# Attention logits of a windowed-attention and gated-MLP kernel summed by accumulating DMAs instead of selector matmuls

## The chip, the cores and the metric

The kernel runs on one core of a Trainium2 chip. The metric is the device time of one execution in microseconds (us). Each kernel was run several times. "Span" is the profiled part of one execution; it is some 2 to 3 us shorter than the time. PE is TensorE, DVE VectorE, ACT ScalarE, POOL GpSimd, SP the engine that issues most DMAs. A name such as L485 is a line of the kernel in question; the line numbers differ from kernel to kernel.

## The reference

```python
# x: 2048 tokens x 640;  32 heads of 20;  window of 8 keys, 2 apart
xn  = layernorm(x)
q, k, v = split_heads(xn @ wqkv)
logits[h, s, w] = sum_d q[h, s, d] * k[h, s - 2*w, d] / sqrt(20)      # -1e9 where s - 2w < 0
attn = softmax(logits, over w)
o[h, s, d] = sum_w attn[h, s, w] * v[h, s - 2*w, d]
out = x + o @ wo + ((xn @ w_gate) * (xn @ w_up)) @ w_down
```

## The kernel before

Tokens lie along the free dimension. The 640 columns of q, k and v are 5 chunks of 128 partitions, permuted so that partition p of every chunk belongs to head p // 4. A head's logit is therefore a sum over 5 chunks and over 4 neighbouring partitions ("head rows"). DVE multiplies q by the shifted k, for two window offsets (a "pair") at a time, and adds two chunks to two others. PE then adds the last three chunks and the four head rows at once, with a 0/1 selector G:

```python
def qk_steps(h, p, s):                 # h: half of the tokens, p: pair of window offsets
    ...                                # prod(): one DVE multiply for both offsets of the pair
    a, b = kept[:, :, 0:NCH - NKC, :], tmp[:]            # NCH = 5 chunks, NKC = 3 stay
    return [ (..., prod(kept, 0, NKC)), (..., prod(tmp, NKC, NCH)), (..., a = a + b on DVE) ]

def qk_logits(h, batch):               # two pairs at a time
    for p, s in batch:
        for c in range(NKC):
            for q in range(NSB):       # 4 blocks of 256 tokens, 32 PSUM partitions each
                e.matmul(PS[32*q:32*q+32, lb, :], G[:], SL[s][:, :, c, q*SB:(q+1)*SB], ...)
    ...                                # ACT copies the bank to LOG, scaled

def attn_move(h):                      # softmax weights back to 128 partitions: 16 DMAs a half
    for r in range(4):
        for q in range(NSB):
            dma(ATB[h][r:128:4, q], LOG[h][32*q:32*q+32])
```

Every engine is one queue, filled once, in program order. While it is built, two counters, `t_pe` and `t_dve`, estimate how far PE and DVE are; the projections, the gated products and the output tiles ("fill") are put between the attention steps by these estimates. `pv(b)` is the attention-times-value work for block b of 256 tokens, on DVE; an output tile t may be queued when `pv(t // 2)` has been:

```python
batch(0, [pair(0, 0), pair(0, 1)]);  batch(0, [pair(0, 2), pair(0, 3)])
...  b0 = pair(1, 0);  softmax head of half 0;  batch(1, [b0, pair(1, 1)]);  softmax rest;  attn_move(0)
batch(1, [pair(1, 2), pair(1, 3)])
pv(0);  settle();  head of softmax 1;  pv(1);  rest of softmax 1;  attn_move(1);  pv(2) ... pv(7)
```

The down-projection weight WD lies in the same memory as the products, so it is loaded only when these have been read. The gated products need USX, a ring of six buffers.

## Time and profile before

| | before |
|---|---|
| time, median of 4 | 262.12 us |
| PE busy / DVE busy, of a span of 260.7 us | 98% / 83% |
| stalls of PE from 31 to 258 us | 0.91 us |
| selector matmuls in the chain | 5.1 us |

The table of engines of the kernel before (busy us, share of the span, instructions), and its slices 2 (tenths of 40 slices of the span; PEclk is the granted clock of PE):

```profile
PE 255.6 (98%) x1669; PEld 150.7 (58%) x1669; DVE 216.1 (83%) x240; ACT 107.3 (41%) x193; POOL 6.7 (3%) x13
...
PE   7999999899999999999999999999999999999996
...
DMA  6968889400000275065001376000311000021301
```

PE is full, or nearly so, from the second slice to the last but one, so only work taken from PE, or a stall, can move the time much. The timeline of PE where the first two groups of selector matmuls stand (start, us, engine, line, what; in brackets the idle time before it and what ended it):

```profile
47.61 0.83 PE L485 MATMUL PS<-SL,G 128*32 128x512 f16 x12
49.35 0.83 PE L485 MATMUL PS<-SL,G 128*32 128x512 f16 x12 [0.91 <-DVE SL L475]
50.11 14.22 PE L424 MATMUL PS<-XNT,WQKV 128*128 128x512 bf16 x65
```

Twelve selector matmuls, placed on four quarters of the array, take only 0.83 us together. The chain that ended last holds them in four pieces (start, us, what):

```profile
49.35 0.83 PE PS L485 x12
...
64.34 1.44 PE PS L485 x24
...
86.41 1.41 PE PS L485 x24
...
110.59 1.41 PE PS L485 x24
```

They sum to 5.1 us; with the stall of 0.91 us, 6.0 us are to be won.

### The profile page before, as it was taken

The numbers are of one execution on the slowest core, as the hardware profiler recorded it, in microseconds if no ns is written. First come the engines' busy times: TensorE is split into PE (matmuls) and PEld (weight loads), VectorE is DVE, ScalarE is ACT, GpSimd is POOL, SyncE is SP. The second block draws the span as 40 slices with busy tenths as digits, with TensorE's granted clock in tenths as the row PEclk, the third lists the DMA queues.
The fourth block names the chain that finished last, engine by engine and source line by source line (L and its number), as shares of the span: only waits on it lengthen the run. The fifth ranks groups of instructions, "written<-read, shape, count | busy, mean of one in ns | idle before, by whom it ended". The sixth has DMA issues, their size and how long they took to land.

```text
span 260.7 us, 4018 instructions
## 1 busy us (share of the span) xinstructions
PE 255.6 (98%) x1669; PEld 150.7 (58%) x1669; DVE 216.1 (83%) x240; ACT 107.3 (41%) x193; POOL 6.7 (3%) x13
## 2 busy tenths in 40 slices
PE   7999999899999999999999999999999999999996
PEld 3899855354554444444467744446774444777775
DVE  5799889999999999998847999999999999422221
ACT  3565558555657555565630035551004555000000
POOL 2000050000200000000000000000000000000000
DMA  6968889400000275065001376000311000021301
GB/s 202 326 136 148 100 226 402 156 3 0 0 3 0 50 206 144 0 208 219 3 0 57 97 199 175 0 4 0 99 54 50 0 3 0 27 74 53 101 28 50
DMA packets 21922, 23.46 MB, mean 90 GB/s; under 512 B 9872, under 2 KB 19472, under 8 KB 21904
## 3 DMA queue, kind: packets, MB, share of 16 engines
q1 hardware_dynamic: 21760, 23.04, 31.2%
q8 instruction: 13, 0.21, 0.3%
q10 hardware_dynamic: 144, 0.16, 0.2%
q14 instruction: 5, 0.04, 0.0%
HBM read 14.42 MB, written 2.62 MB: 65 GB/s over the span
## 4 chain that ended last, share of the span: by engine, by line
PE 80%; DVE 14%; SPq 2%; DMA 2%; ACT 1%; issue 1%
PE PS L577 40%; PE PS L608 28%; PE PS L424 10%; DVE SL L467 3%; SPq L283 2%; DVE XNS L371 2%; PE PS L485 2%; DVE STATS L354 2%; DVE SL L475 2%; DVE TMP L467 2%; DVE STATS L348 2%; DMA XST<-in_A_x_dram 2%; DVE MV L360 1%; DVE SD L369 1%; ACT KH L451 0%
## 5 line engine op out<-in xcount | busy, mean ns | idle before, releaser
L577 PE MATMUL PS<-XNT,WG 128*128 128x512 bf16 x240 | 59.6, 379 | 0.0
L577 PE MATMUL PS<-XNT,WU 128*128 128x512 bf16 x240 | 59.6, 379 | 0.0
L608 PE MATMUL PS<-WD,HT 128*128 128x320 bf16 (+1 forms) x396 | 57.6, 295 | 0.0
L579 ACT ACTIVATE HT<-PS 128x512 bf16<-128x512 f32 x48 | 28.7, 598 | 58.2 <-PE PS L577 58.2
L608 PEld LDWEIGHTS PS<-WD,HT 128*128 128x128 bf16 x396 | 38.1, 98 | 14.7
L551 DVE TENSOR_TENSOR PVB<-VO,ATB 128x10240 f16<-128x10240 bf16 x8 | 43.9, 5488 | 0.1
L424 PE MATMUL PS<-XNT,WQKV 128*128 128x512 bf16 x200 | 43.9, 379 | 0.0
L612 DVE TENSOR_TENSOR FOUT<-PS,XR 128x320 bf16<-128x320 f32 (+1 forms) x33 | 15.5, 477 | 30.4 <-PE PS L608 30.1
L577 PEld LDWEIGHTS PS<-XNT,WU 128*128 128x128 bf16 x240 | 23.4, 98 | 28.5 <-issue 0.4
L577 PEld LDWEIGHTS PS<-XNT,WG 128*128 128x128 bf16 x240 | 23.4, 98 | 28.2 <-issue 0.4
L579 ACT ACTIVATE USX<-PS 128x512 bf16<-128x512 f32 x48 | 28.7, 597 | 22.2 <-PE PS L577 20.8
L424 PEld LDWEIGHTS PS<-XNT,WQKV 128*128 128x128 bf16 x200 | 23.3, 118 | 20.2 <-issue 0.8
L546 DVE TENSOR_TENSOR PVB<-PVB 128x5120 f16<-128x5120 f16 (+1 forms) x16 | 34.4, 2150 | 0.0
L467 DVE TENSOR_TENSOR SL<-QH,KH 128x6144 f16<-128x6144 bf16 x8 | 26.8, 3352 | 1.4 <-ACT KH L451 1.4
L608 PE MATMUL PS<-WO,VO 128*128 128x320 bf16 (+1 forms) x165 | 27.1, 295 | 0.0
L582 DVE TENSOR_TENSOR HT<-HT,USX 128x512 bf16<-128x512 bf16 x48 | 18.5, 417 | 4.2 <-ACT USX L579 4.2
L608 PEld LDWEIGHTS PS<-WO,VO 128*128 128x128 bf16 x165 | 15.9, 98 | 5.9
L475 DVE TENSOR_TENSOR SL<-SL,TMP 128x4096 f16<-128x4096 f16 x8 | 18.3, 2290 | 0.2
L467 DVE TENSOR_TENSOR TMP<-QH,KH 128x4096 f16<-128x4096 bf16 x8 | 18.4, 2302 | 0.0
L430 ACT ACTIVATE VO<-PS 128x512 bf16<-128x512 f32 x20 | 11.9, 597 | 9.8 <-PE PS L424 9.8
L437 PE MATMUL PS<-XNT,WQKV 128*128 128x128 bf16 x200 | 12.6, 220 | 0.2
L437 PEld LDWEIGHTS PS<-XNT,WQKV 128*128 128x128 bf16 x200 | 11.6, 118 | 1.2 <-DVE XNT L394 0.5
(49 smaller groups left out, 137.8 us busy)
## 6 DMA issues: line engine op xcount, KB each, us to landing
ATB<-LOG SPq DMA_DIRECT2D x32, 128.0 KB, 2.6
XR<-in_A_x_dram SPq DMA_DIRECT2D x16, 160.0 KB, 2.3
XST<-in_A_x_dram SPq DMA_DIRECT2D x15, 160.0 KB, 3.9
out_dram<-FOUT SPq DMA_DIRECT2D x15, 160.0 KB, 1.8
WG<-in_B_w_gate_dram SPq DMA_DIRECT2D x1, 1920.0 KB, 9.5
WU<-in_B_w_up_dram SPq DMA_DIRECT2D x1, 1920.0 KB, 13.8
WD<-in_B_w_down_dram SPq DMA_DIRECT2D x1, 1920.0 KB, 8.2
WQKV<-in_A_wqkv_dram SPq DMA_DIRECT2D x10, 160.0 KB, 3.8
```

The lines of the kernel that those rows point to most:

```text
L424: op("pe", (lambda l, x, c: lambda e: e.matmul(PS[:, b, :], l, x, start=(c == 0), stop=(c == NCH - 1)))(l, x, c), r=[l, x], w=[PS[:, b, :] ...
L430: op("act", lambda e: e.activation(o, PS[:, b, :], ACT.Copy), r=[PS[:, b, :]], w=[o], name=f"pev{which}_{m}_{j}")
L437: op("pe", (lambda o, l, x, st, sp: lambda e: e.matmul(o, l, x, start=st, stop=sp))(o, l, x, st, sp), r=[l, x], w=[o], name=f"pp{which}_{m ...
L467: return lambda: op("dve", lambda e: e.tensor_tensor(o[:], qw, kw, ALU.mult), r=[q, k], w=[o[:]], name=f"prod{h}_{p}_{c0}")
L475: lambda: op("dve", lambda e: e.tensor_tensor(a, a, b, ALU.add), r=[a, b], w=[a], name=f"psum{h}_{p}")),
L546: return lambda: op("dve", lambda e: e.tensor_tensor(o, x, y, ALU.add), r=[x, y], w=[o], name=f"{name}_{b}")
L551: lambda: op("dve", lambda e: e.tensor_tensor(PVB[:], vw, aw, ALU.mult), r=[v, a], w=[PVB[:]], name=f"pv_{b}")),
L577: op("pe", (lambda l, x, c: lambda e: e.matmul(PS[:, b, :], l, x, start=(c == 0), stop=(c == NCH - 1)))(l, x, c), r=[l, x], w=[PS[:, b, :] ...
L579: op("act", lambda e: e.activation(o, PS[:, b, :], ACT.Copy), r=[PS[:, b, :]], w=[o], name=f"guev{which}_{m}_{j}")
L582: h_pending.append(lambda: op("dve", lambda e: e.tensor_tensor(h, h, o, ALU.mult), r=[h, o], w=[h], name=f"h{m}_{j}"))
L608: op("pe", (lambda l, x, i, b: lambda e: e.matmul(PS[:, b, 0:wid], l, x, start=(i == 0), stop=(i == n - 1)))(l, x, i, b), r=[l, x], w=[PS[ ...
L612: op("dve", (lambda o, xr, b: lambda e: e.tensor_tensor(o, PS[:, b, 0:wid], xr, ALU.add))(o, xr, b), r=[PS[:, b, :], xr], w=[o], name=f"fi ...
```

## The change

Its intent: free PE of the selector matmuls. DVE writes its products token block by token block in FP16; two accumulating DMAs of 512 KB add chunks to the first product; a plain copy of head row 0 and three accumulating DMAs of head rows 1 to 3 (128 KB each) build the logits, now 32 heads times 4 token blocks on 128 partitions. Each of the six must wait for the one before. The weights go back by 4 DMAs a half with a repeated source. The attention scale moves into the copy of q, the mask becomes an addition, and the softmax is FP16. The diff, cut to its core:

```diff
-    NKC = 3
-    NSL = 3
-    SL = [sb(f"SL{s}", [128, 2, NKC, HS], FP16) for s in range(NSL)]
+    PSB = [128, NSB, 2, SB]
+    PP = [sb(f"PP{s}", [128, 2] + PSB[1:], FP16, at=a_pr + ...) for s in range(2)]   # in WD's memory
+    PE_ = [ five buffers for the first product, three of them in PVB's memory ]
...
-        return [ prod(kept, 0, NKC), prod(tmp, NKC, NCH), a + b ]          # 2 multiplies
+        return prod(first, 4, 1) + prod(a, 0, 2) + prod(b, 2, 2) + [ a + b ]   # 6 multiplies
+    def acc(o, i, name):
+        op("pool", lambda e: e.dma_start(o, i, accum_op=ALU.add), r=[o, i], w=[o], dma=True, name=name)
+    def qk_chain(h, p, s, en):
+        return [
+            lambda: acc(first[:], slot[:, 0], f"acc{h}_{p}_0"),
+            lambda: acc(first[:], slot[:, 1], f"acc{h}_{p}_1"),
+            lambda: dma(dst, row(0), r=[first[:]], w=[dst], name=f"row{h}_{p}_0"),
+            lambda: acc(dst, row(1), f"row{h}_{p}_1"),
+            lambda: acc(dst, row(2), f"row{h}_{p}_2"),
+            lambda: acc(dst, row(3), f"row{h}_{p}_3"),
+        ]
-    def qk_logits(h, batch):   ... selector matmuls, LOG evictions, mask ...
...
     def pair(h, p):
         ... DVE steps ...
+        ch[0]();  held[0]();  ch[1]();  held[1]()        # held: rows 2 and 3 of the pair before
+        ch[2]();  ch[3]();    held[:] = ch[4:]
...
     pv(0)
-    settle()
+    pv(1)
+    settle(b_end + 15.0)
     for it in headB: step(it)
-    pv(1)
     for it in restB: step(it)
```

More of the change, by code (lines that the diff above doesn't have):

```diff
@@ L26 @@
 EPS = 1e-5
-NEG = -1e9
+NEG = -30000.0
 VP = 32
@@ L232, in build_kernel @@
     a_pr = place[0]
-    NKC = 3
-    NSL = 3
-    WD = sb("WD", [128, NF, D], at=a_pr)
-    WO = sb("WO", [128, NCH, D], at=a_pr + NF * D * 2)
-    SL = [sb(f"SL{s}", [128, 2, NKC, HS], FP16) for s in range(NSL)]
-    PVB = sb("PVB", [128, NCH, W, SB], FP16, at=place[0] - 2 * NKC * HS * 2)
-    TMP = sb("TMP", [128, 2, NCH - NKC, HS], FP16)
+    WD = sb("WD", [128, NF, D])
+    WO = sb("WO", [128, NCH, D])
+    PSB = [128, NSB, 2, SB]
+    PP = [sb(f"PP{s}", [128, 2] + PSB[1:], FP16, at=a_pr + 2 * s * HS * 4) for s in range(2)]
+    PE_ = [sb("PE0", PSB, FP16, at=a_pr + 4 * HS * 4)]
+    a_pv = place[0]
+    PVB = sb("PVB", [128, NCH, W, SB], FP16)
+    TMP = sb("TMP", [128, 2] + PSB[1:], FP16, at=a_pv)
+    for s in range(3):
+        PE_.append(sb(f"PE{s + 1}", PSB, FP16, at=a_pv + (2 + s) * HS * 4))
     XNT = sb("XNT", [128, NCH, S])
@@ L243, in build_kernel @@
     for h in range(2):
-        ATB.append(sb(f"ATB{h}", [128, NSB, W, SB], at=place[0]))
+        ATB.append(sb(f"ATB{h}", [128, NSB, W, SB], FP16, at=place[0]))
+        if h == 0:
+            PE_.append(sb("PE4", PSB, FP16, at=place[0] + NSB * W * SB * 2))
         QH.append(sb(f"QH{h}", [128, NCH, HS]))
@@ L250, in build_kernel @@
     a_log = place[0]
-    LOG = [sb(f"LOG{h}", [128, W, SB]) for h in range(2)]
-    M1 = sb("M1", [128, 4, SB])
-    M2 = sb("M2", [128, 2, SB])
-    M3 = sb("M3", [128, SB])
+    LOG = [sb(f"LOG{h}", [128, W, SB], FP16) for h in range(2)]
+    M1 = sb("M1", [128, 4, SB], FP16)
+    M2 = sb("M2", [128, 2, SB], FP16)
+    M3 = sb("M3", [128, SB], FP16)
     S1 = sb("S1", [128, 4, SB], FP16)
@@ L276, in build_kernel @@
     IDENT = sb("IDENT", [128, 128])
-    G = sb("G", [128, H], FP16)
+    MASK = sb("MASK", [128, W, PAD], FP16)
+    MSK0 = sb("MSK0", [128, W, PAD], FP16)
     PS = nc.alloc_psum_tensor("PS", [128, 8, 512], FP32)
@@ L291, in build_kernel @@
        r=[IDENT[:]], w=[IDENT[:]], name="ident")
-    op("pool", lambda e: e.memset(G[:], 0.0), w=[G[:]], name="g0")
-    op("pool", lambda e: e.affine_select(G[:], G[:], pattern=[[-4, H]], compare_op=ALU.is_gt,
-                                         fill=1.0, base=-3, channel_multiplier=1),
-       r=[G[:]], w=[G[:]], name="g1")
-    op("pool", lambda e: e.affine_select(G[:], G[:], pattern=[[-4, H]], compare_op=ALU.is_ge,
-                                         fill=0.0, base=0, channel_multiplier=1),
-       r=[G[:]], w=[G[:]], name="g2")
     op("pool", lambda e: e.memset(KH[0][:, :, 0:PAD], 0.0), w=[KH[0][:, :, 0:PAD]], name="kpad")
     op("pool", lambda e: e.memset(VO[:, :, 0:VP], 0.0), w=[VO[:, :, 0:VP]], name="vpad")
+    op("pool", lambda e: e.memset(MASK[:], 0.0), w=[MASK[:]], name="mask0")
+    op("pool", lambda e: e.memset(MSK0[:], 0.0), w=[MSK0[:]], name="msk0")
+    op("pool", lambda e: e.affine_select(MSK0[:], MSK0[:], pattern=[[DIL, W], [1, PAD]], compare_op=ALU.is_ge, fill=NEG,
+                                         base=-PAD, channel_multiplier=0), r=[MSK0[:]], w=[MSK0[:]], name="msk1")
     def x_load(t, eng="sp"):
@@ L326, in late_loads @@
     def late_loads():
+        dma(MASK[0:128:4], MSK0[0:32], r=[MSK0[0:32]], w=[MASK[0:128:4]], name="mask")
         wqkv_load(2)
@@ L429, in proj @@
             o = qk_dst(which, m, j * JB, JB)
-        op("act", lambda e: e.activation(o, PS[:, b, :], ACT.Copy), r=[PS[:, b, :]], w=[o], name=f"pev{which}_{m}_{j}")
+        sc = SCALE if which == 0 else 1.0
+        op("act", lambda e: e.activation(o, PS[:, b, :], ACT.Copy, scale=sc), r=[PS[:, b, :]], w=[o],
+           name=f"pev{which}_{m}_{j}")
     def proj_part(which, t, ms, b, col):
@@ L450, in part_evac @@
         i = PS[:, b, col:col + nm * nt * TS].rearrange("p (m s) -> p m s", m=nm)
-        op("act", lambda e: e.activation(o, i, ACT.Copy), r=[PS[:, b, :]], w=[o], name=f"ppev{which}_{m0}_{t0}")
+        sc = SCALE if which == 0 else 1.0
+        op("act", lambda e: e.activation(o, i, ACT.Copy, scale=sc), r=[PS[:, b, :]], w=[o], name=f"ppev{which}_{m0}_{t0}")
     def k_seam():
@@ L455, in k_seam, with qk_steps @@
         op("pool", lambda e: e.tensor_copy(o, i), r=[i], w=[o], name="kseam")
-    def qk_steps(h, p, s):
-        kept, tmp = SL[s], TMP
+    def qk_steps(h, p, s, en):
+        slot, first = PP[s], PE_[en]
         kp = KH[h][:, 0, 0:1].ap[0]
-        def prod(o, c0, c1):
-            q = QH[h][:, c0:c1, :]
-            k = KH[h][:, c0:c1, 4 * p:4 * p + HS + 2]
-            kw = bass.AP(k.tensor, k.offset, [kp, [2, 2], [KL, c1 - c0], [1, HS]])
-            qw = q.unsqueeze(1).to_broadcast([128, 2, c1 - c0, HS])
-            return lambda: op("dve", lambda e: e.tensor_tensor(o[:], qw, kw, ALU.mult), r=[q, k], w=[o[:]],
-                              name=f"prod{h}_{p}_{c0}")
-        a, b = kept[:, :, 0:NCH - NKC, :], tmp[:]
-        return [
-            (0.16 + 2 * NKC * HS / 1920, prod(kept, 0, NKC)),
-            (0.16 + 2 * (NCH - NKC) * HS / 1920, prod(tmp, NKC, NCH)),
-            (0.16 + 2 * (NCH - NKC) * HS / 1920,
-             lambda: op("dve", lambda e: e.tensor_tensor(a, a, b, ALU.add), r=[a, b], w=[a], name=f"psum{h}_{p}")),
-        ]
@@ L478, in qk_logits @@
-    def qk_logits(h, batch):
-        for p, s in batch:
-            lb = 6 + p % 2
-            for c in range(NKC):
-                for q in range(NSB):
-                    o = PS[32 * q:32 * q + 32, lb, :]
-                    x = SL[s][:, :, c, q * SB:(q + 1) * SB]
-                    op("pe", (lambda o, x, q, c: lambda e: e.matmul(o, G[:], x, start=(c == 0), stop=(c == NKC - 1),
-                                                                 tile_position=(0, 32 * q)))(o, x, q, c),
-                       r=[G[:], x], w=[o], name=f"lg{h}_{p}_{c}_{q}")
-        for p, s in batch:
-            lb = 6 + p % 2
-            o = LOG[h][:, 2 * p:2 * p + 2, :]
-            i = PS[:, lb, :].rearrange("p (w s) -> p w s", w=2)
-            op("act", (lambda o, i: lambda e: e.activation(o, i, ACT.Copy, scale=SCALE))(o, i),
-               r=[PS[:, lb, :]], w=[o], name=f"lgev{h}_{p}")
-        if h == 0 and batch[-1][0] == 3:
-            m = LOG[0][0:32, :, 0:PAD]
-            op("pool", lambda e: e.affine_select(m, m, pattern=[[DIL, W], [1, PAD]], compare_op=ALU.is_ge, fill=NEG,
-                                                 base=-PAD, channel_multiplier=0), r=[m], w=[m], name="mask")
@@ new lines, in prod @@
+        def prod(o, c0, n):
+            out = []
+            for w in range(2):
+                q = QH[h][:, c0:c0 + n, :]
+                k = KH[h][:, c0:c0 + n, 4 * p + 2 * w:4 * p + 2 * w + HS]
+                ow = bass.AP(o.tensor, o.offset + w * SB, [o.ap[0], [2 * HS, n], [2 * SB, NSB], [1, SB]])
+                qw = q.rearrange("p c (q s) -> p c q s", q=NSB)
+                kw = k.rearrange("p c (q s) -> p c q s", q=NSB)
+                out.append((0.16 + n * HS / 1920, (lambda ow, qw, kw: lambda: op(
+                    "dve", lambda e: e.tensor_tensor(ow, qw, kw, ALU.mult), r=[qw, kw], w=[ow],
+                    name=f"prod{h}_{p}_{c0}"))(ow, qw, kw)))
+            return out
@@ new lines, in qk_steps, with row @@
+        a, b = slot[:], TMP[:]
+        return prod(first[:], NCH - 1, 1) + prod(a, 0, 2) + prod(b, 2, 2) + [
+            (2.3, lambda: op("dve", lambda e: e.tensor_tensor(a, a, b, ALU.add), r=[a, b], w=[a], name=f"psum{h}_{p}")),
+        ]
+    def acc(o, i, name):
+        op("pool", lambda e: e.dma_start(o, i, accum_op=ALU.add), r=[o, i], w=[o], dma=True, name=name)
+    def qk_chain(h, p, s, en):
+        slot, first = PP[s], PE_[en]
+        dst = LOG[h][:, 2 * p:2 * p + 2, :]
+        def row(r):
+            x = first[r:128:4]
+            return bass.AP(x.tensor, x.offset, [x.ap[0], [2 * SB, NSB], [1, 2 * SB]])
+        return [
+            lambda: acc(first[:], slot[:, 0], f"acc{h}_{p}_0"),
[4 more added lines that the diff above has]
+            lambda: acc(dst, row(3), f"row{h}_{p}_3"),
+        ]
@@ L510, in recip @@
                 return e.reciprocal(RS[:], S3[:])
-        head = [
+        first = LOG[h][:, :, 0:PAD]
+        head = [(0.25, tt(first, first, MASK[:], ALU.add, "mask"))] if h == 0 else []
+        head += [
             (0.7, tt(M1[:], L[:, 0:4], L[:, 4:8], ALU.max, "smax1")),
@@ L530, in attn_move @@
     def attn_move(h):
-        for r in range(4):
-            for q in range(NSB):
-                src, dst = LOG[h][32 * q:32 * q + 32], ATB[h][r:128:4, q]
-                dma(dst, src, r=[src], w=[dst], name=f"atb{h}_{q}_{r}", group=("atb", h))
+        for q in range(NSB):
+            x, dst = LOG[h][q:128:4], ATB[h][:, q]
+            src = bass.AP(x.tensor, x.offset, [x.ap[0], [0, 4], [1, W * SB]])
+            dma(dst, src, r=[x], w=[dst], name=f"atb{h}_{q}")
     def pv_steps(b):
@@ L697, in build_kernel @@
     k_seam()
-    bank_ring[:] = [b for b in bank_ring if b < 6]
     def exp_preload():
@@ L705, in build_kernel @@
     pv_done = [0]
-    batches = []
     loaded = []
@@ L736, in build_kernel, with run_fill @@
     add_dn(3)
-    def take():
-        h, batch, at = batches.pop(0)
-        qk_logits(h, batch)
-        t_pe[0] = max(t_pe[0], at) + 0.44 + 0.2175 * NKC * len(batch)
-        if h == 1 and batch[-1][0] == 3:
-            down_loads()
-            out_loads()
-            loaded.append(True)
-    def run_fill(until, upto=None):
+    def run_fill(until):
         while t_pe[0] < until and pos[0] < len(fill):
-            if batches and t_pe[0] >= batches[0][2]:
-                take()
-                continue
             it = fill[pos[0]]
@@ L763, in run_fill @@
             pos[0] += 1
-        while batches and (t_pe[0] >= batches[0][2] or until >= batches[0][2]):
-            take()
     def force_fill(n):
@@ L774, in step, with settle @@
         run_fill(t_dve[0])
-    slot = [0]
+    held = []
     def pair(h, p):
-        s = slot[0] % NSL
-        slot[0] += 1
-        assert all(s != x for _, ps, _ in batches for _, x in ps)
-        for it in qk_steps(h, p, s):
+        n = 4 * h + p
+        en = (1, 2, 3, 1, 2, 3, 0, 4)[n]
+        for it in qk_steps(h, p, n % 2, en):
             step(it)
-        return p, s
-    def batch(h, pairs):
-        batches.append((h, pairs, t_dve[0] + 0.3))
-    def settle():
-        while batches:
-            run_fill(batches[0][2] + 0.01)
-        t_dve[0] = max(t_dve[0], t_pe[0] + 1.6)
-    batch(0, [pair(0, 0), pair(0, 1)])
-    batch(0, [pair(0, 2), pair(0, 3)])
+        ch = qk_chain(h, p, n % 2, en)
+        ch[0]()
+        for f in held[0:1]:
+            f()
+        ch[1]()
+        for f in held[1:]:
+            f()
+        ch[2]()
+        ch[3]()
+        held[:] = ch[4:]
+    def settle(lag):
+        t_dve[0] = max(t_dve[0], lag)
+    for p in range(4):
+        pair(0, p)
+    a_end = t_dve[0]
     headA, restA = softmax_steps(0)
@@ L798, in build_kernel @@
     t_dve[0] = max(t_dve[0], t_pe[0] + 0.8)
-    b0 = pair(1, 0)
-    settle()
+    pair(1, 0)
+    pair(1, 1)
+    settle(a_end + 15.0)
     for it in headA:
         step(it)
-    batch(1, [b0, pair(1, 1)])
+    t_dve[0] += 1.6
     for it in restA:
@@ L806, in build_kernel @@
     attn_move(0)
-    batch(1, [pair(1, 2), pair(1, 3)])
+    pair(1, 2)
+    pair(1, 3)
+    b_end = t_dve[0]
+    for f in held:
+        f()
+    down_loads()
+    out_loads()
+    loaded.append(True)
     for t in range(NXR):
@@ L819, in build_kernel @@
     pv(0)
-    settle()
+    pv(1)
+    settle(b_end + 15.0)
     for it in headB:
         step(it)
-    bank_ring[:] = bank_ring + [6, 7]
-    pv(1)
+    t_dve[0] += 1.6
     for it in restB:
```

## The prediction

> **What bounds the kernel now.** TensorE. In the page's table of engines PE is busy 98% of 260.7 us; in the chain of waits PE's lines hold 80%, and before 31 us stands the layer norm on DVE, which the change leaves alone. From 31 to 258 us PE stalls once, 0.91 us ahead of the second group of selector matmuls. DVE is busy 83% but has slack: by its timeline the last attention output (VO) is written at 222.5 us and needed near 250.
>
> **What the change removes.** The 96 selector matmuls: 0.83+1.44+1.41+1.41 = 5.1 us of the chain, and the 0.9 us stall. Eight LOG evictions on ACT (4.8 us) were not critical. If everything added hides, 262.1 - 6.0 = 256.1 us, 2.3% less: hardly over the 2% line.
>
> **What it adds and moves.** DVE: a pair of window offsets took 3.35+2.30+2.29 us. It becomes two products of 1024 elements (0.69 each, as the 1024-element max), four of 2048 (1.22 each), and the same 2.29 us sum: about 8.5 instead of 7.9, 5 us in all, inside DVE's slack. Fewer attention copies (0.6 us of issue each): not critical.
>
> The real addition is a serial DMA chain per pair: two accumulates of 512 KB, a 128 KB row copy, three 128 KB row accumulates, each waiting for the one before, five of six on one in-order queue. The Trainium skill ("DMA: Bandwidth & Descriptors", Anatomy of one DMA) puts a GpSimd-issued DMA at about 2.0 us plus bytes/436 GB/s; no such DMA runs in this trace, but plain 128 KB copies between tiles land in 2.6 us by the list of issues. For 512 KB that gives 3.2 us, about 4.4 if the accumulate's second read doubles the traffic (estimate). With the earlier pair's steps interleaved, a pair's period is two large accumulates + a row copy + about 1 us of issue: 10 us at 3.2, 12.4 at 4.4, 14 at 5. DVE makes a pair in 8.5, so the queue sets the pace.
>
> **What then is critical.** The first chain starts near 42 us. With a 4.4 us accumulate the fourth pair's logits are complete near 100 us, where DVE wants them at 83; DVE then sits in order before the gated products (HT), the six USX buffers run out, and PE stalls 5 to 8 us near 95 to 105. The eighth pair's second accumulate ends near 140; only then may WD be loaded (same memory; 8.2 us), where PE wants it at 127. Together 15 to 20 us of stall against 6 saved: about 272 us. At 3.2 us nearly all hides (256 to 258); at 5 it is 285.
>
> **Prediction:** 272 us, 8 in 10 between 256 and 292. Faster by over 2%: 0.22; within 2%: 0.20; slower by over 2%: 0.58.
>
> **What would show each step.** Selector matmuls gone. In the list of issues, large accumulates take 4 us or more to landing, row accumulates about 3. DVE waits for DMAs before products from the third pair on and before the first max. PE waits before the first WD matmul, for WD's DMA or for DVE. PE busy falls 6 us while the span grows.
>
> **What would make it wrong.** Large accumulates at 3.3 us or less: the chains keep pace, 256 to 258. Accumulates much slower than a copy (7 us): above 300. Or descriptor writing on GpSimd held up by DVE's products, as the KH copy seems to be (70 elements, 3.4 us, beside a DVE product).

## More of the kernel before

The timeline of DVE shows where the second attention block (its 5.5 us product, then its result VO) stood against the first output eviction (FOUT):

```profile
122.92 5.48 DVE L551 TENSOR_TENSOR PVB<-VO,ATB 128x10240 f16<-128x10240 bf16 x1
...
134.95 0.49 DVE L612 TENSOR_TENSOR FOUT<-PS,XR 128x320 bf16<-128x320 f32 x1 [1.25 <-PE PS L608]
...
142.29 0.81 DVE L546 TENSOR_TENSOR VO<-PVB 128x1280 bf16<-128x1280 f16 x1
```

The product is queued 12 us ahead of the first eviction.

## The result, and the profile after

The changed kernel takes 301.61 us (median of 4, 301.34 to 302.43) against 262.12 us: a ratio of 1.151 (95% interval 1.148 to 1.153). The predicted direction is right; the size, 39.5 us instead of 10, lies outside the range.

The table of engines and slices of the changed kernel:

```profile
PE 257.1 (86%) x1558; PEld 151.3 (51%) x1573; DVE 218.5 (73%) x273; ACT 102.4 (34%) x185; POOL 37.1 (12%) x52
...
PE   8999999999998207999305939999999999999996
...
PEclk9999999999999755999955877999999999999999
DMA  7788799476866668865889210224011200004121
```

PE has holes where it had none; near them its granted clock falls to half; the DMA engines, idle in many of these slices before, are busy to some two thirds through the first half. One sign that the prediction named did not come: PE's busy time was to fall by 6 us and rose from 255.6 to 257.1, because slow matmuls count as busy time. The timeline of PE gives every stall of the middle part:

```profile
102.52 2.31 PE L587 MATMUL PS<-XNT,WU 128*128 128x512 bf16 x5 [6.36 <-ACT USX L589]
113.95 2.31 PE L587 MATMUL PS<-XNT,WG 128*128 128x512 bf16 x5 [9.12 <-ACT HT L589]
...
120.37 1.24 PE L587 MATMUL PS<-XNT,WG 128*128 128x512 bf16 x5
...
160.36 3.36 PE L618 MATMUL PS<-WD,HT 128*128 128x320 bf16 x12 [16.08 <-DMA WD<-in_B_w_down_dram]
...
179.79 1.51 PE L618 MATMUL PS<-WO,VO 128*128 128x320 bf16 x5 [5.65 <-DVE VO L556]
```

The four waits are 6.36 + 9.12 + 16.08 + 5.65 = 37.2 us. The first matmuls after each wait run at half speed: five take 2.31 us where five take 1.24 at full clock. Summed over the slow groups this is 7.7 us. Waits and slow clock are 44.9 us; minus the 6.0 us saved, 38.9 us, which is the growth of the span (38.1) within a microsecond. So the loss is fully placed. The timeline of POOL, which issues the accumulates, shows what stands behind the first three waits:

```profile
41.76 0.99 POOL L488 DMA_DIRECT2D PE<-PP  x1 [7.73 <-DVE PP L484]
51.18 0.86 POOL L488 DMA_DIRECT2D PE<-PP  x1 [8.43 <-DMA PE<-PP]
59.19 0.87 POOL L488 DMA_DIRECT2D LOG<-PE  x1 [7.15 <-DMA LOG<-PE]
59.72 1.21 POOL L488 DMA_DIRECT2D PE<-PP  x1
62.18 0.86 POOL L488 DMA_DIRECT2D LOG<-PE  x1 [1.24 <-DMA LOG<-PE]
64.96 0.86 POOL L488 DMA_DIRECT2D PE<-PP  x1 [1.92 <-DMA PE<-PP]
65.91 0.86 POOL L488 DMA_DIRECT2D LOG<-PE  x1
71.84 0.88 POOL L488 DMA_DIRECT2D LOG<-PE  x1 [5.07 <-DMA LOG<-PE]
72.38 1.21 POOL L488 DMA_DIRECT2D PE<-PP  x1
```

PE<-PP is a large accumulate (the tile is called PE; it is not the engine), LOG<-PE a row. The next pair's first large accumulate (59.72, 72.38) stands right behind row 1 (59.19, 71.84), which waits for the row copy, which waits for the second large accumulate. A pair thus occupies the queue for 12.7 us; DVE needs 8.1 (the spacing when nothing holds it, in no_rows below). The first and second pair are even 18.0 us apart. The list of DMA issues of the changed kernel (KB of one, median us from issue to landing):

```profile
PE<-PP POOLq DMA_DIRECT2D x16, 512.0 KB, 4.8
...
LOG<-PE POOLq DMA_DIRECT2D x24, 128.0 KB, 3.5
...
LOG<-PE SPq DMA_DIRECT2D x8, 128.0 KB, 2.1
```

The Trainium skill ("DMA: Bandwidth & Descriptors", Anatomy of one DMA) gives about 2.0 us plus bytes over 436 GB/s for a DMA issued from GpSimd: by estimate 3.2 and 2.3 us for these sizes. The accumulates measured 4.8 and 3.5. That the steps must be waited for one by one is what the same page says (Two DMAs through the same engine are not ordered): only the completion semaphore orders them (no run here leaves such a wait out).

The timeline of DVE shows the fourth stall:

```profile
151.32 1.09 DVE L592 TENSOR_TENSOR HT<-HT,USX 128x512 bf16<-128x512 bf16 x3
165.09 0.49 DVE L622 TENSOR_TENSOR FOUT<-PS,XR 128x320 bf16<-128x320 f32 x1 [12.68 <-PE PS L618]
167.93 0.49 DVE L622 TENSOR_TENSOR FOUT<-PS,XR 128x320 bf16<-128x320 f32 x1 [2.35 <-PE PS L618]
168.34 5.48 DVE L561 TENSOR_TENSOR PVB<-VO,ATB 128x10240 f16<-128x10240 bf16 x1
```

DVE stands idle for 12.7 us with the second attention block ready to run, because that block is queued behind two evictions of output tiles, and these wait for WD. Before, the block came 12 us ahead of the first eviction. Once the evictions are through, PE has to wait for the block.

### The profile page after: what moved, and what is told of

Read it like the earlier page. It is cut to its first block, busy times and chain, and to the rows that moved or that the text cites. A ratio compares the mean times of both kernels' runs of the same rounds, so it can differ in the third digit from the quotient of the medians.

```text
span 298.8 us, 3851 instructions
## 1 busy us (share of the span) xinstructions
PE 257.1 (86%) x1558; PEld 151.3 (51%) x1573; DVE 218.5 (73%) x273; ACT 102.4 (34%) x185; POOL 37.1 (12%) x52
## 3 DMA queue, kind: packets, MB, share of 16 engines
q0 software_dynamic: 5760, 11.54, 22.1%
## 4 chain that ended last, share of the span: by engine, by line
PE 41%; DMA 32%; DVE 19%; issue 2%; SPq 2%; ACT 1%; POOL 1%
PE PS L618 24%; DMA PE<-PP 22%; PE PS L587 17%; DMA LOG<-PE 5%; DMA WD<-in_B_w_down_dram 3%; SPq L289 2%; DVE PVB L561 2%; DVE XNS L375 2%; DVE STATS L358 2%; DVE TMP L478 2%; DVE PP L478 2%; DVE PP L484 2%; DVE STATS L352 1%; DVE PVB L556 1%; DMA XST<-in_A_x_dram 1%
## 5 line engine op out<-in xcount | busy, mean ns | idle before, releaser
L618 PE MATMUL PS<-WD,HT 128*128 128x320 bf16 (+1 forms) x396 | 60.7, 305 | 16.1 <-DMA WD<-in_B_w_down_dram 16.1
L587 PE MATMUL PS<-XNT,WU 128*128 128x512 bf16 x240 | 61.8, 389 | 6.4 <-ACT USX L589 6.4
L618 PE MATMUL PS<-WO,VO 128*128 128x320 bf16 (+1 forms) x165 | 28.5, 305 | 5.7 <-DVE VO L556 5.7
L428 PEld LDWEIGHTS PS<-XNT,WQKV 128*128 128x128 bf16 x200 | 23.5, 118 | 19.5
L488 POOL DMA_DIRECT2D LOG<-PE x24 | 21.1, 880 | 60.0 <-DMA LOG<-PE 59.5
L478 DVE TENSOR_TENSOR PE<-QH,KH 128x1024 f16<-128x1024 bf16 x16 | 10.4, 689 | 18.0 <-DMA LOG<-PE 16.6
L618 PEld LDWEIGHTS PS<-WO,VO 128*128 128x128 bf16 x165 | 16.3, 101 | 12.4 <-DVE VO L556 6.0
L478 DVE TENSOR_TENSOR PP<-QH,KH 128x2048 f16<-128x2048 bf16 x16 | 18.9, 1218 | 5.0 <-DMA PE<-PP 5.0
L488 POOL DMA_DIRECT2D PE<-PP x16 | 15.9, 993 | 36.4 <-DMA PE<-PP 23.7
L478 DVE TENSOR_TENSOR TMP<-QH,KH 128x2048 f16<-128x2048 bf16 x16 | 19.0, 1217 | 0.0
L484 DVE TENSOR_TENSOR PP<-PP,TMP 128x4096 f16<-128x4096 f16 x8 | 18.3, 2289 | 0.2
## 6 DMA issues: line engine op xcount, KB each, us to landing
WU<-in_B_w_up_dram SPq DMA_DIRECT2D x1, 1920.0 KB, 16.3
```

What stands on the lines that cost most here:

```text
L428: op("pe", (lambda l, x, c: lambda e: e.matmul(PS[:, b, :], l, x, start=(c == 0), stop=(c == NCH - 1)))(l, x, c), r=[l, x], w=[PS[:, b, :] ...
L478: "dve", lambda e: e.tensor_tensor(ow, qw, kw, ALU.mult), r=[qw, kw], w=[ow],
L484: (2.3, lambda: op("dve", lambda e: e.tensor_tensor(a, a, b, ALU.add), r=[a, b], w=[a], name=f"psum{h}_{p}")),
L488: op("pool", lambda e: e.dma_start(o, i, accum_op=ALU.add), r=[o, i], w=[o], dma=True, name=name)
L587: op("pe", (lambda l, x, c: lambda e: e.matmul(PS[:, b, :], l, x, start=(c == 0), stop=(c == NCH - 1)))(l, x, c), r=[l, x], w=[PS[:, b, :] ...
L618: op("pe", (lambda l, x, i, b: lambda e: e.matmul(PS[:, b, 0:wid], l, x, start=(i == 0), stop=(i == n - 1)))(l, x, i, b), r=[l, x], w=[PS[ ...
```

## The experiments

Theory A: the loss is the serial chain of DMAs, through latency in one in-order queue. Rival B: DVE's longer work and the new order of instructions. Rival C: the throughput of the 16 DMA engines. The sixteen kernels were run in four groups, each group on one chip with the kernel before beside it (its median there was 262.1 to 262.4 us). "wrong" marks a result that is wrong on purpose.

| run | us | ratio to before (95%) |
|---|---|---|
| changed kernel | 301.6 | 1.148 to 1.153 |
| copy_only (wrong) | 264.3 | 1.006 to 1.009 |
| no_large (wrong) | 264.4 | 1.006 to 1.009 |
| no_rows (wrong) | 276.4 | 1.051 to 1.056 |
| half_bytes (wrong) | 283.8 | 1.080 to 1.086 |
| reorder | 304.6 | 1.158 to 1.163 |
| reorder2 | 298.6 | 1.137 to 1.144 |
| pv1_first | 293.4 | 1.116 to 1.124 |
| reorder2_pv1 | 289.9 | 1.104 to 1.109 |
| early_weights | 306.4 | 1.166 to 1.170 |
| keep_warm | 300.5 | 1.141 to 1.147 |
| copy_only_pv1 (wrong) | 258.0 | 0.983 to 0.986 |
| before_split | 267.0 | 1.017 to 1.019 |
| before_copies4 | 262.3 | 0.999 to 1.002 |
| hyb0 | 261.3 | 0.995 to 0.998 |
| hyb1 | 260.0 | 0.991 to 0.993 |
| hyb2 | 264.4 | 1.008 to 1.013 |

### How much is the chain: copy_only, no_large, no_rows

```diff
-        ch[0]();  held[0]();  ch[1]();  held[1]();  ch[2]();  ch[3]();  held[:] = ch[4:]
+        ch[2]()                                        # copy_only: the plain row copy alone
+        held...;  ch[2]();  ch[3]();  held[:] = ch[4:] # no_large: rows only
+        ch[0]();  ch[1]();  ch[2]()                    # no_rows: large ones and the copy only
```

> The changed kernel with all 40 accumulating DMAs left out; only the plain row copy of each pair stays (results wrong on purpose). Theory A (the serial DMA chain and its latency make the loss): the time falls from 301.6 to 256-264 us; what then remains over 256 is DVE's extra product time before the first down-projection tiles. Rival B (the split DVE products and the new order of instructions make the loss): it stays above 285 us.

> The two 512 KB accumulates of each pair left out, the row copy and the three row accumulates kept with their lag of one pair (wrong on purpose). Theory A in its form 'the two large ones in series with the row copy set the period of 12.7 us': the rows alone fit under DVE's 8.1 us a pair, so 257-266 us. If the three row steps matter as much as the large ones: 275 us or more.

> The three row accumulates of each pair left out, the two large ones and the row copy kept (wrong on purpose). If the coupling in the in-order queue is what stretches the period (a row accumulate waits for the row copy, and the next pair's first accumulate stands behind it), the period falls from 12.7 to DVE's pace or near 9 us and the time to 262-275 us. If the two large accumulates alone set the pace by their latency or by the DMA engines' throughput, the period stays at 10 us or more and the time above 278 us.

Without accumulates the time is 264.3 us, so 37 of the loss go with them and B cannot be the main cause; but 264.3 is just outside the 256 to 264 expected, is not the 256 the prediction allowed, and is slower than before. The rows alone cost nothing more (264.4). The large ones alone cost 12 us (276.4, just outside the 262 to 275 expected). Both together cost 37: the two do not add, each makes the other dearer. This run takes away both the rows' place in the queue and their traffic; half_bytes, below, tells the two apart. In no_rows POOL is free to issue the next pair's first large accumulate while the row copy is under way, and in the undisturbed stretch of its POOL timeline these start 8.1 to 8.5 us apart (62.88, 70.96, 79.49), DVE's own pace, instead of 12.7. What remains there is the end of the row: the eighth pair's second large accumulate still has to land before WD may be loaded. The timeline of PE in no_rows:

```profile
136.02 3.29 PE L618 MATMUL PS<-WD,HT 128*128 128x320 bf16 x12 [10.75 <-DMA WD<-in_B_w_down_dram]
...
154.19 1.51 PE L618 MATMUL PS<-WO,VO 128*128 128x320 bf16 x5 [5.65 <-DVE VO L556]
```

The waits for USX are gone, the ones for WD and VO are not.

### Is it the order in the queue: reorder, reorder2

```diff
+        ch[0]();  R3(n-2);  R1(n-1);  ch[1]();  R2(n-1);  ch[2]()     # reorder
+        ch[0]();  R1(n-1);  ch[1]();  R2(n-1);  R3(n-1);  ch[2]()     # reorder2
```

> The same 48 DMAs and a right result, queued so that each accumulate's predecessor has had time to land: large 1 of pair n, row 3 of n-2, row 1 of n-1, large 2 of n, row 2 of n-1. Theory A with the queue order as the cause: period 9 to 10 us instead of 12.7, first max about 98 instead of 108 us, time 275-288 us. Rival C (the 16 DMA engines' throughput sets the period: they are busy two thirds of that stretch already): landings grow as the order tightens, the period stays above 11.5 us and the time above 293 us.

> The changed kernel, right result, same DMAs; the first row accumulate of a pair is queued behind the NEXT pair's first large accumulate, so that the next chain no longer stands behind a wait for this pair's row copy; rows 2 and 3 follow the next pair's second large accumulate. In the first reordering the rows came a pair later still, and DVE waited for the three first-product buffers. If the place of that one wait in the queue sets the period: 10 to 11 us instead of 12.7, first max near 100 instead of 108 us, time 284-294 us. If the DMA engines' throughput sets it: no gain, 298 us or more.

Both missed, and both came out where rival C was expected (a period of 14 us and 304.6 us in the one; 298.6 us in the other). Their traces say more. reorder lost 3 us: the rows come so late that DVE waits 19.8 us in all (16.6 in the changed kernel) for the three first-product buffers in use, and in the later part its first accumulates stand 14 us apart (79.33, 93.20, 107.26). reorder2 won 3 us: 11.5 us apart instead of 12.7, not the 10 to 11 expected. Its POOL still waits for landings one after the other, 3.2, 1.4 and 2.6 us in one period (before the issues at 84.87, 87.10 and 90.59), because rows 2 and 3 now stand in a row. And the list of DMA issues of reorder2 shows longer landings:

```profile
PE<-PP POOLq DMA_DIRECT2D x16, 512.0 KB, 5.0
...
LOG<-PE POOLq DMA_DIRECT2D x24, 128.0 KB, 4.2
```

Overlapping a row with a large accumulate stretches the row from 3.5 to 4.2 us. So C has a part. In the changed kernel the queue of POOL's DMAs took 22.1% of 16 engines' span; 22.1% of 298.8 us over 8 pairs is 8.3 us of all 16 engines a pair (an estimate), as much as DVE's 8.1. By it a better order has little below 8.3 us to go to; no order that was tried came near it.

### Latency or bytes, slope or offset: half_bytes

```diff
-            lambda: acc(first[:], slot[:, 0], ...)
+            lambda: acc(first[:, 0:2], slot[:, 0, 0:2], ...)      # both large ones: half the columns
```

> The changed kernel with the two large accumulates of a pair cut to half of the columns (256 KB each, wrong on purpose), the number and order of all DMAs unchanged. From the two sizes measured (4.8 us for 512 KB, 3.5 for 128 KB) the landing should be 3.9 to 4.0 us, the period 12.7 minus 1.7 = 11 us. If the loss follows the landing at the prediction's own slope of 16 us per us: 301.6 - 13 = 287 to 290 us; the step that failed is then an offset. If bytes are all that counts (the prediction's formula at half size): 262 to 270 us. If the fixed part rules wholly: 297 us or more.

The large ones landed in 3.5 us, below the 3.9 expected, and the rows in 2.7:

```profile
PE<-PP POOLq DMA_DIRECT2D x16, 256.0 KB, 3.5
...
LOG<-PE POOLq DMA_DIRECT2D x24, 128.0 KB, 2.7
```

The time, 283.8 us, lies below the 287 to 290 expected. It fell by 17.8 us for 1.3 us of landing: 13.7 us per us. The prediction's own figures give 12.5 per us between 3.2 and 4.4 us and 21.7 above, so the measured slope is of that size, though part of the gain is that of the rows, which also landed 0.8 us sooner. But at 3.5 us they give 261 us and the chip gave 283.8; at the true 4.8 us they give 281 and the chip gave 301.6. An offset of 21 to 23 us is missing at both sizes.

This run also answers rival C. The timeline of POOL in half_bytes (first accumulates of three pairs):

```profile
55.73 1.21 POOL L488 DMA_DIRECT2D PE<-PP  x1
...
66.38 1.21 POOL L488 DMA_DIRECT2D PE<-PP  x1
...
76.49 1.21 POOL L488 DMA_DIRECT2D PE<-PP  x1
```

The pairs come 10.1 to 10.8 us apart. POOL's DMAs took 16.3% of 16 engines' span of 281.3 us, by estimate 5.7 us of all 16 a pair. In no_rows they took 5.5 us a pair, and the pairs came 8.1 to 8.5 us apart, although a large accumulate took longer to land there (4.5 us). So at nearly the same load on the engines it is the rows in the one in-order queue that stretch the period. The prediction's own sum for a period (two large landings, the row copy, 1 us of issue) gives 10.0 us here and 12.7 for the changed kernel with the landings measured.

### Where the offset comes from: pv1_first, copy_only_pv1, early_weights, keep_warm

```diff
-                fill.append(("dn", t // 2, 2.31, ...))            # output tile t needs pv(t // 2)
+                fill.append(("dn", max(t // 2, 1), 2.31, ...))    # pv1_first, copy_only_pv1
```

> The changed kernel with the second attention block queued on DVE ahead of the evictions of the first two output tiles. Theory: the 5.7 us wait of PE for VO near 174-180 us comes from DVE's in-order queue (12.7 us idle behind an eviction whose matmuls wait for WD), not from lack of time. Expected 293-296 us. Rival: DVE has no room there, no change (301).

> The changed kernel without its accumulating DMAs (wrong on purpose), and with the second attention block queued on DVE ahead of the first output tiles' evictions. Without the second edit it took 264.3 us, 8 us over the 256 that the removal of the selector matmuls allows. If those 8 us are the place of the attention block in DVE's queue: 257 to 259.5 us. If they are the time of the six-instruction products (DVE full until then): 262 us or more.

One number in the rule that queues the output tiles is worth 8.2 us: 293.4, as expected. The wait for VO is gone. Without accumulates, too, it brings 264.3 to 258.0, within 2 us of the 256.1 that the prediction worked out. So the six-instruction products do fit into DVE's time, as predicted; what had failed was the order on DVE. The diff moves `pv(1)` ahead of the second softmax, but the time estimates put two output tiles ahead of it, and the prediction did not work this out. With the order mended in both, the accumulates cost 293.4 - 258.0 = 35.4 us.

```diff
+        if t == 9: gu_loads()         # early_weights: WG and WU some 10 us sooner
```

> The changed kernel with WG and WU (3.8 MB) loaded some 10 us earlier, so that the first accumulate (9.1 us to landing beside them, 4.5 to 5 later) meets less traffic. If that contention shifts the whole row of chains: first chain 4 us shorter, time 294-299 us. If it is absorbed by later waits: 300-302 us. A slower layer norm at the start would show as a later first product (33.2 us now).

This missed, and it is confounded: the early loads held up the transposing DMAs of the layer norm, and the first product started at 42.1 instead of 33.2 us. Its POOL timeline still answers the question:

```profile
50.60 0.99 POOL L492 DMA_DIRECT2D PE<-PP  x1 [7.73 <-DVE PP L488]
55.56 0.86 POOL L492 DMA_DIRECT2D PE<-PP  x1 [3.96 <-DMA PE<-PP]
62.45 0.87 POOL L492 DMA_DIRECT2D LOG<-PE  x1 [6.03 <-DMA LOG<-PE]
62.98 1.21 POOL L492 DMA_DIRECT2D PE<-PP  x1
```

With no weights in flight the first two chains are 12.4 us apart, not 18.0. The kernel started its products 8.8 us late and ended 4.8 us late, so the contention costs about 4 us in the changed kernel. That is inferred, as no run has the one without the other.

```diff
+        if (t, nb) == (0, 0): keep_warm(64)    # 64 dummy matmuls where PE waits for WD
```

> The changed kernel with 64 dummy matmuls of about 0.216 us ahead of the first matmul on WD, where PE waits 16.1 us for a DMA. If the slow matmuls after that wait (3.36 us for twelve instead of 1.79) come from PE's granted clock after an idle stretch, they run at full speed and the time falls by 2 to 3.5 us, to 298-300 us; the same test says that the rest of the loss is waiting. No change: the slow matmuls have another cause.

The first matmuls on WD in the timeline of PE of keep_warm:

```profile
144.39 14.10 PE L606 MATMUL PS<-ZERO 128*128 128x512 bf16 x64
160.75 1.79 PE L627 MATMUL PS<-WD,HT 128*128 128x320 bf16 x12 [2.26 <-DMA WD<-in_B_w_down_dram]
```

They take 1.79 us, full speed, instead of 3.36. So the slow groups are the granted clock after idleness, and busy work removes them. The Trainium skill ("TensorE: Matmul & The Clock Gate", Part 1: The HAM clock gate) says that PE falls to half rate after an idle window of about 3.4 us and needs about as long to return; the traces here agree: waits of 3.4 us (hyb2, below) and more were followed by groups at half speed, waits of 2.3 us and less were not. The time won, 1.2 us (300.5, just outside the 298 to 300 expected), is less than the 2.9 that the groups after WD had lost: WD landed 0.4 us later, the wait for VO that follows stayed at 5.65 us, and the slow stretch after it was longer (3.41 us for the next twelve on WD, 2.77 in the changed kernel). That the dummy matmuls made it longer is not shown: the same twelve take 3.41 us in copy_only, with no cold start shortly before, and in no_rows, with one.

> The second queue order (298.6 us alone) and the attention block moved (293.4 us alone) together, right result. If the two waits are separate, the gains of 3 and 8 us add: 289.5 to 292 us. If one hides behind the other: 293 us or more.

reorder2 and pv1_first together gave 289.9 us: 3.0 + 8.2 = 11.2 us if they add, 11.7 measured. The two are separate causes.

### The other parts of the change alone: before_copies4, before_split

```diff
+            src = bass.AP(x.tensor, x.offset, [x.ap[0], [0, 4], [1, W * SB]])   # before_copies4
+            for w in range(2): ... one multiply for each offset, chunks 1 + 2 + 2   # before_split
```

> The kernel before, with only the attention copies changed: 4 DMAs of 512 KB for each half in place of 16 of 128 KB (right result). The copies are off the critical path in every theory: within 0.3% of before.

> The kernel before, with only the products split as the change splits them (six instructions for a pair in place of two, same elements; right result). DVE has 3 to 5 us more to do before the first attention blocks. If that has slack, as the prediction said: within 0.5 us of before. If DVE has none in that stretch: 264 to 266 us.

The four copies change nothing, as every theory said. The split products cost 4.9 us in the kernel before, more than either expectation allowed (267.0 us). This looks like "DVE has no time"; copy_only_pv1, where the same split products fit, speaks against that reading. The timeline of DVE in before_split shows the same slip as in the changed kernel:

```profile
129.58 0.43 DVE L582 TENSOR_TENSOR HT<-HT,USX 128x512 bf16<-128x512 bf16 x1 [1.73 <-ACT USX L579]
131.74 0.43 DVE L582 TENSOR_TENSOR HT<-HT,USX 128x512 bf16<-128x512 bf16 x1 [1.73 <-ACT USX L579]
133.42 0.49 DVE L612 TENSOR_TENSOR FOUT<-PS,XR 128x320 bf16<-128x320 f32 x1 [1.25 <-PE PS L608]
133.82 5.48 DVE L551 TENSOR_TENSOR PVB<-VO,ATB 128x10240 f16<-128x10240 bf16 x1
```

DVE idles again and again before 133 us, and the block's product stands behind the eviction instead of 12 us ahead of it. The split changed the durations in `t_dve`, the estimates placed the block later, and PE waited 3.6 us for it. This is read from the trace; no run has the split products with the block first in the kernel before.

### A version that beats both: hyb0, hyb1, hyb2

The runs point to two things: the block's place on DVE, and an accumulate that has 5 us to spare. hyb0 is the kernel before with the block first and the selector matmuls queued 1 us later. hyb1 adds one accumulate for each of the last six pairs (chunk 1 onto chunk 0) and so drops 24 selector matmuls. hyb2 uses two in a row for the second half.

```diff
+    def qk_acc(h, p, s):
+        for k in range(1, NACC[4*h + p] + 1):        # hyb1: [0,0,1,1,1,1,1,1]  hyb2: [0,0,1,1,2,2,2,2]
+            dma_start(SL[s][:, :, 0, :], SL[s][:, :, k, :], accum_op=ALU.add)      # on POOL
-            for c in range(NKC):
+            for c in [0] + list(range(1 + NACC[4*h + p], NKC)):
-        batches.append((h, pairs, t_dve[0] + 0.3))
+        batches.append((h, pairs, t_dve[0] + (1.3 or 6.5; hyb2 7.0)))
+    pv(0); pv(1); settle(); head of softmax 1; pv(2); rest of softmax 1; ...
```

> hyb1 without its accumulates: the kernel before with only the attention block moved and the selector matmuls queued 1 us later. If hyb1's 2.1 us come from 24 fewer matmuls (1.4 us) and the removed stall (0.9 us): 261 to 261.6 us here. If the order on DVE did it all: 260 us.

> The kernel before with the accumulate used only where it has time: for the last six pairs ONE accumulating DMA adds chunk 1 to chunk 0, and the selector matmul takes two chunks instead of three (24 matmuls fewer); the matmuls of a batch are queued later; the second attention block comes ahead of the second softmax and of the first output tiles. Right result. Expected: 1.4 us of matmuls and the 0.9 us stall gone, 259.5 to 261 us (0.5 to 1% under before). If a 5 us landing delays WD or the logits: 262 us or more.

> hyb1 with two accumulates, one after the other, for each of the four pairs of the second half (16 more matmuls gone, 1 us). If the longer chains still hide: 259 to 259.6 us. If they delay the load of WD, as in the change: 261 us or more.

hyb0 took 261.3 us, as expected: the 0.9 us stall is gone from its timeline. hyb1 took 260.0 us, right result, 0.8% under the kernel before with an interval that excludes 1, though within the 2% that is called the same here. The further 1.25 us is close to the 1.4 us that 24 selector matmuls took. hyb2 missed. Two landings in a row take 10 us, more than the 7 allowed for, and PE waits in its queue, by its timeline:

```profile
95.90 0.57 PE L494 MATMUL PS<-SL,G 128*32 128x512 f16 x4 [3.40 <-DMA SL<-SL]
```

One accumulate under other work is a small gain, two in series already a loss.

## Why the prediction was right or wrong

- **What bounds the kernel, and what is saved: right.** The selector matmuls are gone, PE was what bounded the kernel, and the most that could be won was 6.0 us. copy_only_pv1, 258.0 us, comes within 2 us of the 256.1 worked out.
- **The queue sets the pace: right.** 12.4 us a pair was given for a landing of 4.4; measured were 12.7 and 4.8 (rows 3.5 for "about 3"). That the periods agree so well is partly luck: by the prediction's sum a landing of 4.8 us gives 13.2, but the row copy took 2.1 us and not 2.6.
- **The places of the stalls: right.** USX near 95 to 105 us (measured 96 to 114), then WD before the first down-projection matmul, were named; both are there.
- **Their size: wrong.** "Together 15 to 20 us of stall" is the step that failed: PE waited 31.6 us at the two places named, and two further terms stand below. The USX stalls were 15.5 us, not 5 to 8, because the fourth pair's logits were first read at 108.3 us, not 100. Of these 8.3 us, some 5.6 come from the first chain, which was given the same period as the others though the weights were loading beside it (18.0 us to the second chain instead of 12.4; in the time of the kernel about 4 us, inferred from early_weights). Some 2.5 come from the fourth chain itself, which took 23.3 us from its first accumulate (84.99) to the first read instead of the 20.8 that the prediction's figures leave: landings were longer, and rows 2 and 3 stand behind the next pair's large accumulates. WD's wait was 16.1 us; WD was issued at 151.5 us, where the prediction had the eighth pair's second accumulate end near 140, and PE came to it late as well (144.3 instead of 127).
- **Two terms were not in the sum at all.** The wait for VO, with its slow matmuls, is 7.3 us by the trace (5.65 + 1.65) and 8.2 us by pv1_first. It comes from the order on DVE. "Inside DVE's slack" was true of time and false of order. The clock after the other idle stretches is about 6 us, read from the slow groups; keep_warm shows the cause, and got back 1.2 us of it.
- **The sum.** 31.6 + 7.3 + 6.1 = 45 us of stall and slow clock stand against the 15 to 20 predicted; that is 25 to 30 us more, and the time was 29.6 over. The landing (4.8 us for 4.4) is a small part of this: at the prediction's own slope it would be 9 us, but the period grew by 0.3 us only. Put as the offset of half_bytes, 8.2 (VO) + about 4 (weights) + about 6 (clock) make 18 of the 21 us; the rest stays open, and the shares are rough (in pv1_first the clock after the other waits cost 4 us, not 6).
- **Not at work:** DVE's products holding up POOL's descriptor writing, which the prediction named as a risk. A POOL issue takes 0.84 to 0.99 us, 1.21 right behind another, whatever DVE does.

## What to carry to other kernels

Before replacing cheap work on the bounding engine (here 0.83 us of matmuls a pair) with a chain of dependent DMAs, multiply the landing of one by the length of the chain, ask how many chains one in-order queue can interleave, and only then look at bytes. When a kernel's queues are filled by time estimates, a change of a single duration can move another step behind a wait: work out the new order on each engine, not only the durations. And add to each predicted stall of the matmul engine the slow clock that follows it (here after waits of 3.4 us and more).

## What the Trainium skill lacked or had wrong

- "DMA: Bandwidth & Descriptors", Anatomy of one DMA: the formula for a GpSimd-issued DMA gives, as an estimate, 3.2 us for 512 KB and 2.3 us for 128 KB. An accumulating DMA within SBUF took 4.8 and 3.5 us (median), 2.1 us for a plain 128 KB copy from SP. The page has no figure for accumulates.
- Same page, no section: what accumulates cost the 16 engines. The share of POOL's queue gives by estimate 2.8 us of all 16 for 512 KB (no_rows: 16.1% of 274.2 us over 16 accumulates), more than half of the landing; rows beside large ones stretched from 3.5 to 4.2 us.
- "SBUF — State Buffer", Who interferes with whom: a DVE instruction with two SBUF inputs blocks a GpSimd instruction that reads SBUF, and descriptor generation is inferred to be unaffected. Both agree here: a 70-element copy on POOL took 3.43 us beside a 3.36 us product and 0.76 us beside a 0.69 us one; the DMA issues kept to about 0.9 us beside such products.
- "TensorE: Matmul & The Clock Gate", Part 1: agrees (half speed after waits of 3.4 us and more). How long the slow stretch lasts varied here: after the same 5.65 us wait, twelve matmuls on WD took 2.56 us in half_bytes, 2.77 in the changed kernel and 3.41 in keep_warm, copy_only and no_rows (1.79 at full speed). No run shows what sets this.
